# Splitting keys and values into float16 parts 1024 columns at a time

## The chip, the cores and the metric

The kernel runs on one core of a Trainium2 chip. The metric is the device time of one execution in microseconds; the time before is the median of three runs, 798.39 us (798.29 to 798.98).

## The reference

Block-sparse attention over four batches, eight heads, 768 positions and a head size of 64, followed by a gated MLP on the 3072 resulting tokens of 512 features. Each 32-row block of queries sees its neighbour blocks, the first and last block, and three drawn blocks; the first and last query blocks see everything. Cut to what matters:

```python
scores = scale * np.matmul(q, k.transpose(0, 1, 3, 2))
scores = np.where(mask, scores, -1000000000.0)
attn = softmax(scores)                     # with max subtracted, + 1e-09 in the divisor
x = np.matmul(attn, v)                     # heads joined: (3072, 512)
g = x @ w_gate                             # 512 -> 1536
out = (g * sigmoid(g) * (x @ w_val)) @ w_out   # 1536 -> 512
```

All inputs and the output are float32.

## The kernel before

TensorE multiplies float16. So every float32 operand is scaled by a power of two and split into two float16 parts: ACT writes the high part, `hi = scale * x` rounded to float16 (`hi_part`, line 391), and DVE the low part, `lo = scale * x - hi` (`lo_part`, line 394). A product is then three matmuls: high by high, high by low and low by high. Batch 0 and the first two of nine chunks of the MLP go in float32 as they are; batches 1 to 3 and the other chunks go in parts.

The work is staged so: while TensorE does the attention of batch 0 and its MLP chunks, ACT and DVE split the MLP's weights in place, `w1t` (gate and value) and `w2all` (output), one tile of 512 columns after the other (`split_w`). In a weight split the ACT instruction writes over what the split before it has still to read, so it waits for the DVE instruction of that split: the weight splits are a chain ACT, DVE, ACT, DVE. For each batch 1 to 3 `load_kv` then runs twice, for the values and for the keys:

- three loads of 256 tokens each into the buffer `stage` (four slots of 1024 float32 columns; a slot holds two tiles of 128 tokens by 512 columns), issued by the SP queue;
- a sum of squares on ACT (line 398), a matmul that sums it over the partitions (`nrm_v` or `nrm_k`, line 388), and on DVE the power-of-two scale (`vs` or `ks`);
- for each of three slots `i`, and in it for each of two halves `tt` of 512 columns, `high` on ACT and `low` on DVE. The parts of slot 0 go into the fourth slot, those of slot 1 into the slot that held the raw data of slot 0, and so on, so slot `i + 1` can be split only when slot `i` is done;
- values: one store of each split slot into a buffer in DRAM, `vd`, from which the attention gathers its rows. Keys: for each half a DMA that transposes it into `kst` (line 739), both issued by SP. DVE copies the key blocks of a query block from `kst` into `kring` (lines 1112 to 1115) ahead of its scores (`qk`, line 1137).

The attention of a block is a chain over all engines: scores on TensorE, maximum and mask on DVE (line 1151), exponential on ACT (line 1168), high and low parts of the probabilities (`pp`), a transposing DMA (`pts`, line 1193), the product with the values (`pv`, line 1206). TensorE fills the time between with matmuls of the MLP: `p` (line 1693, or 1687 in float32) and `po` (line 1756).

The order on each engine is set ahead. Every step is added to a `Plan` as a task with an engine, an estimated time, the tasks it needs, and a rank (shifted by a table, `SHIFT`); `Plan.order` plays the tasks through once with these estimates, and the instructions are emitted in that order. Each engine carries out its own instructions strictly in this order, waiting where it must. The tasks `high` and `low` of both halves stay in the plan with the estimates they had, so the order of tasks is the same with and without the change.

Of the kernel before, what the change touches and what calls it, by code (L numbers as in the profile page):

```python
# [17 lines left out]
B, H, S, D = 4, 8, 768, 64  # L18
# [101 lines left out]
class Plan:  # L120
# [9 lines left out]
    def add(self, eng, us, emit, need=(), rank=0.0, take=(), use=(), dma=None, behind=None, late=0.0, many=1):  # L130
        t = Task()
        t.late, t.many = late, many if dma is not None and eng != "POOL" else 0
        t.eng, t.us, t.emit, t.take, t.dma = eng, us, emit, list(take), dma
        t.key = self.key if rank > -50.0 else ""
        t.rank = rank + SHIFT.get(t.key, 0.0)
        t.need = [x for x in need if x is not None]
        t.outs, t.next, t.ready, t.end, t.no = [], [], 0.0, None, len(self.tasks)
        t.left = len(t.need) + (behind is not None)
        if behind is not None:
            behind.next.append(t)  # L140
        for x in t.need:
            x.outs.append(t)
        for b in list(take) + list(use):
            b.users.append(t)
        self.tasks.append(t)
        return t
# [81 lines left out]
def tile_block_sparse_attn_swiglu(  # L228
# [55 lines left out]
    def get(buf, name):  # L284
        if buf.ring in given:
            n = given[buf.ring]
            given[buf.ring] += 1
            buf.tile = stage[:, n % 4, :]
            return buf.tile
        pool, shape, dt, n = KINDS[buf.ring]  # L290
        buf.tile = pool.tile(shape, dt, tag=buf.ring, name=name, bufs=n)
        return buf.tile
# [97 lines left out]
    def hi_part(hi, src, scale):  # L390
        nc.scalar.activation(hi, src, AF.Copy, scale=scale)  # L391

    def lo_part(lo, src, scale, hi):
        nc.vector.scalar_tensor_tensor(lo, src, scale, hi, op0=ALU.mult, op1=ALU.subtract)  # L394
# [254 lines left out]
    def load_kv(b, what, rank, need):  # L649
# [4 lines left out]
        sc = {}  # L654
        raws, loads = [], []
# [41 lines left out]
        t = add("PE", 0.12, norm, sq, rank, take=[n])  # L697
        t = add("DVE", 0.7, scale, [t], EVAC, use=[n])
# [3 lines left out]
            bt.vsc, bt.vsc_t = sc, t  # L702
            bt.vd = dram.tile([S, 2 * DM], F16, tag="vd", name=f"vd_{b}")

        def views(i, tt):

            dst = parts[i].tile.bitcast(F16)
            pat = "p (t h l d) -> p t h l d" if what == "k" else "p (t l h d) -> p t h l d"
            dst = dst.rearrange(pat, h=H, l=2, d=D)
            return dst[:, tt, :, 0, :], dst[:, tt, :, 1, :], raws[i][1]().rearrange("p t (h d) -> p t h d", d=D)[:, tt]  # L710

        done = []
        for i in range(3):
            los = []
            for tt in range(2):

                def high(i=i, tt=tt):
                    if i and not tt:
                        get(parts[i], f"{what}16_{b}_{i}")
                    hi, _, s = views(i, tt)  # L720
                    hi_part(hi, s, sc["s"][:, 0:1])

                def low(i=i, tt=tt):
                    hi, lo, s = views(i, tt)
                    lo_part(lo, s, sc["s"][:, 0:1], hi)

                ru = [raws[i][0]]
                first = i > 0 and tt == 0
                pi = parts[i : i + 1]
                h_ = add("ACT", 0.63, high, [t] + los, rank, take=pi if first else [], use=ru + ([] if first else pi))  # L730
                l_ = add("DVE", 0.68, low, [h_], rank, use=ru + pi)
                los.append(l_)
                if what == "k":

                    def turn(i=i, tt=tt):
                        if i == 0 and tt == 0:
                            get(bt.ks, f"kst_{b}")
                        tok = (2 * i + tt) * P
                        nc.sync.dma_start_transpose(
                            bt.ks.tile[:, :, tok : tok + P],  # L740
                            parts[i].tile.bitcast(F16)[:, tt * 1024 : (tt + 1) * 1024],
                        )

                    f0 = i == 0 and tt == 0
                    done.append(add("SP", 1.3, turn, [l_], rank, behind=None if f0 else done[0], take=[bt.ks] if f0 else [],
                                    use=pi + ([] if f0 else [bt.ks]), dma=1.7))
            if what == "v":

                def put(i=i):
                    nc.sync.dma_start(  # L750
                        bt.vd[i * 256 : (i + 1) * 256, :].rearrange("(t p) n -> p t n", p=P),
                        parts[i].tile.bitcast(F16).rearrange("p (t n) -> p t n", t=2),
                    )

                done.append(add("SP", 0.5, put, los, rank, use=parts[i : i + 1], dma=1.6))
# [1099 lines left out]
```

## Time and profile before

| | |
|---|---|
| median of 3 runs | 798.39 us |
| profiled execution | 800.0 us, span 798.2 us |
| TensorE (PE) | 762.4 us busy, 96% of the span |
| VectorE (DVE) | 547.4 us, 69% |
| ScalarE (ACT) | 504.5 us, 63% |
| GpSimd (POOL) | 205.7 us, 26% |
| granted TensorE clock | 0.99 of full speed |
| splits of keys and values of batches 1 to 3 | 36 instructions on ACT, 36 on DVE, 25.2 and 27.2 us |

A row of the timeline reads: start in us from the span's start, duration in us, engine, line of the kernel, operation, output and inputs by the program's names, shapes, count, and in brackets the idle time of the engine before it with what ended it. A row of the groups gives count, busy time in us and the mean of one in ns, then idle time ahead of it. A row of the waits gives who waited for whom, the total in us, the number of times, and the longest. Matmuls overlap in TensorE's pipeline, so being busy is not the same as running at full rate.

### The profile page before, as it was taken

How to read it: one execution, taken by the hardware profiler on the slowest of the kernel's cores; microseconds unless marked ns; L12 is line 12 of the kernel's file. 1: busy time of each engine (PE TensorE's matmuls, PEld its weight loads, DVE VectorE, ACT ScalarE, POOL GpSimd, SP SyncE). 2: the span in 40 equal slices, each digit the busy share in tenths (PEclk: the TensorE clock that was granted, in tenths of full speed). 3: DMA queues.
4: the chain of work that ended last, by engine and by line, in shares of the span. 5: the costliest groups of instructions: out<-in, count | busy, mean ns of one | idle time of the engine just before them, and what ended most of it. 6: DMA issues, size and time to landing. Idle time of an engine off the chain costs nothing.

```text
span 798.2 us, 21196 instructions
## 1 busy us (share of the span) xinstructions
PE 762.4 (96%) x8098; PEld 489.2 (61%) x8098; DVE 547.4 (69%) x1658; ACT 504.5 (63%) x1211; POOL 205.7 (26%) x257
## 2 busy tenths in 40 slices
PE   3789999999999999999999999999999999999998
PEld 2557778884587566645665566645665566555655
DVE  5676898998898787742799866753798767731220
ACT  2687767587688686763598856754487757641221
POOL 3553511322033223201223222401223233101210
PEclk9889999999999999999999999999999999999999
DMA  8963537647877979478769994947878974330001
GB/s 205 259 220 118 193 146 260 205 125 230 198 151 172 212 169 197 91 197 265 159 134 182 269 227 114 203 97 211 188 133 179 228 177 105 69 69 19 1 1 39
DMA packets 171430, 128.08 MB, mean 160 GB/s; under 512 B 115008, under 2 KB 136896, under 8 KB 171328
## 3 DMA queue, kind: packets, MB, share of 16 engines
q1 hardware_dynamic: 165696, 109.42, 56.6%
q0 software_dynamic: 5632, 17.31, 8.5%
q8 instruction: 63, 1.03, 0.5%
q14 instruction: 39, 0.32, 0.1%
HBM read 79.50 MB, written 11.01 MB: 113 GB/s over the span
## 4 chain that ended last, share of the span: by engine, by line
PE 63%; DVE 18%; DMA 8%; issue 4%; ACT 4%; SPq 1%; DVEq 1%; ACTq 0%
PE p L1693 29%; PE po L1756 18%; PE pv L1206 4%; PE p L1687 3%; DMA q<-in_q_dram 3%; PE qk L1137 3%; DVE pp L394 2%; DVE act L1702 1%; DVE act L1707 1%; DMA pts<-pp 1%; DVE w1t L394 1%; DVE e L1151 1%; DMA stage<-in_k_dram 1%; DVE kring L1114 1%; PE qk L1341 1%
## 5 line engine op out<-in xcount | busy, mean ns | idle before, releaser
L1693 PE MATMUL p<-xall,w1t 128*128 128x384 f16 (+1 forms) x2016 | 326.8, 319 | 0.0
L1693 PEld LDWEIGHTS <-w1t 128*128 128x128 f16 x2016 | 191.2, 98 | 115.5 <-issue 8.5
L1715 POOL TENSOR_TENSOR h<-act,h 128x384 f16<-128x384 f32 (+1 forms) x108 | 101.6, 941 | 372.5 <-ACT h L1712 372.1
L1756 PE MATMUL po<-w2all,h 128*128 128x512 f16 (+1 forms) x900 | 195.3, 371 | 0.3 <-DVE w2all L394 0.3
L1756 PEld LDWEIGHTS <-h 128*128 128x128 f16 x900 | 84.6, 98 | 93.7 <-issue 5.6
L1712 ACT CAST h<-act 128x384 f16<-128x384 f32 (+1 forms) x108 | 50.8, 471 | 82.5 <-DVE act L1707 82.2
L1124 POOL DMA_INDIRECT w2all<-vd,vidx x66 | 62.8, 951 | 150.2 <-PE pv L1206 126.7
L1702 DVE SCALAR_TENSOR_TENSOR act<-act,p 128x384 f32<-128x384 f32 (+1 forms) x108 | 54.2, 504 | 65.2 <-ACT act L1698 64.5
L1687 PE MATMUL p<-xall,w1t 128*128 128x256 f32 x384 | 88.8, 384 | 0.4 <-DVE act L1702 0.3
L1168 ACT ACTIVATE e<-e,nb,es 128x256 f32<-128x256 f32 x132 | 78.2, 593 | 2.2
L1687 PEld LDWEIGHTS p<-xall,w1t 128*128 128x128 f32 x384 | 71.4, 192 | 12.0 <-DVE w2all L394 1.4
L1698 ACT ACTIVATE act<-p,gsc 128x384 f32<-128x384 f32 (+1 forms) x84 | 47.0, 560 | 31.2 <-PE p L1693 30.6
L1707 DVE SCALAR_TENSOR_TENSOR act<-act,hs,p 128x384 f32<-128x384 f32 (+1 forms) x84 | 49.7, 591 | 21.8 <-PE p L1693 18.8
L1206 PEld LDWEIGHTS <-w2all 128*128 128x128 f16 x1584 | 55.1, 98 | 13.9 <-issue 3.8
L394 DVE SCALAR_TENSOR_TENSOR pp<-e,rr,pp 128x256 f16<-128x256 f32 x132 | 61.2, 510 | 1.3 <-ACT pp L391 1.0
L391 ACT ACTIVATE pp<-e,rr 128x256 f16<-128x256 f32 x132 | 58.1, 496 | 3.7 <-DVE rr L782 2.5
L1206 PE MATMUL pv<-pts,w2all 128*128 128x64 f16 x1584 | 57.0, 193 | 2.8 <-DMA pts<-pp 2.8
L1151 DVE CUSTOM_DVE_ANT_1 e<-qk,msk 128x256 f32<-128x256 f32 x132 | 50.0, 417 | 2.8 <-issue 2.4
L1593 ACT ACTIVATE ot<-po,oc 128x512 f32<-128x512 f32 (+1 forms) x25 | 16.7, 667 | 42.9 <-PE po L1756 42.7
L1114 DVE COPY kring<-kst 128x256 f16 x198 | 38.9, 251 | 5.6 <-PE qk L1137 5.3
L1232 DVE TENSOR_TENSOR xall<-pv,xall 64x256 f16<-64x256 f32 x66 | 27.7, 420 | 21.1 <-ACT xall L1227 18.7
L1137 PE MATMUL qk<-kring,qs 128*32 128x256 f16 x1056 | 35.7, 274 | 0.2 <-DVE mx L1151 0.2
(187 smaller groups left out, 899.4 us busy)
## 6 DMA issues: line engine op xcount, KB each, us to landing
stage<-in_w_dram SPq DMA_DIRECT2D x36, 512.0 KB
w2all<-vd SPq DMA_DIRECT2D x66, 192.0 KB
qs<-qraw SPq DMA_DIRECT2D x72, 128.0 KB
out_dram<-ot SPq DMA_DIRECT2D x19, 256.0 KB
qn<-in_q_dram SPq DMA_DIRECT2D x36, 128.0 KB
qraw<-in_q_dram SPq DMA_DIRECT2D x36, 128.0 KB
stage<-in_v_dram SPq DMA_DIRECT2D x9, 512.0 KB
vd<-stage SPq DMA_DIRECT2D x9, 512.0 KB
```

Of the source, the lines that this page charges most:

```text
L391: nc.scalar.activation(hi, src, AF.Copy, scale=scale)
L394: nc.vector.scalar_tensor_tensor(lo, src, scale, hi, op0=ALU.mult, op1=ALU.subtract)
L1124: nc.gpsimd.indirect_dma_start(vf[0:96, 1, :], None, bt.vd, bass.IndirectOffsetOnAxis(ap=vidx[0:96, qb : qb + 1], axis=0))
L1137: nc.tensor.matmul(stv[u * BLK : (u + 1) * BLK, g].rearrange("p s k -> p (s k)"), o.q[:, l, h // 2, h % 2, col : col + BLK], kg[:, h].rear ...
L1151: nc.vector.tensor_tensor_reduce(ev[:, g], stv[:, g], o.g.msk[:, qb, :].unsqueeze(2).broadcast_to([P, 8, BLK]), scale=1.0, scalar=-3.0e38, ...
L1168: nc.scalar.activation(ev[:, g], ev[:, g], AF.Exp, bias=nb_[:, g : g + 1], scale=o.g.es[:, 0:1], accum_out=c["rs"][:, g : g + 1],)
L1206: nc.tensor.matmul(pvv[:, j, n % 2], vg[:, cc, l, 2 * j : 2 * j + 2, :], pq[:, g, m, cc, u : u + 2, :], start=i == 0, stop=i == 5,)
L1687: nc.tensor.matmul(t[:, 0:tc_], w[:, i + 1, k_ * P : (k_ + 1) * P], x_k(k_), start=k_ == 0, stop=k_ == NKT - 1)
L1693: nc.tensor.matmul(t[:, 0:tc_], w_[:, f, m, k_, :], x_k(k_, l), start=i == 0, stop=i == 11)
L1702: nc.vector.scalar_tensor_tensor(a_, a_, 1.0, pg.tile[:, 0:tc_], op0=ALU.add, op1=ALU.mult)
L1715: nc.gpsimd.tensor_tensor(hv(f)[:, 1, :], act.tile[:, 0:tc_], hv(f)[:, 0, :], op=ALU.subtract)
L1756: nc.tensor.matmul(po.tile[:, cs], hv(f)[:, l, ts_], w2h[:, f, m, cs], start=f == 0 and i == 0, stop=f == NF - 1 and i == 2)
```

## The change

`high` and `low` of the first half now take the whole slot, 1024 columns in one instruction; those of the second half emit nothing. The transposes and stores stay where they were, as do all other instructions. On SP the second transpose of a slot needs no wait of its own on DVE any more, since the first one has waited for the whole slot.

```diff
-        def views(i, tt):
+        def views(i):
...
-            return dst[:, tt, :, 0, :], dst[:, tt, :, 1, :], raws[i][1]().rearrange("p t (h d) -> p t h d", d=D)[:, tt]
+            return dst[:, :, :, 0, :], dst[:, :, :, 1, :], raws[i][1]().rearrange("p t (h d) -> p t h d", d=D)
...
                 def high(i=i, tt=tt):
                     if i and not tt:
                         get(parts[i], f"{what}16_{b}_{i}")
-                    hi, _, s = views(i, tt)
-                    hi_part(hi, s, sc["s"][:, 0:1])
+                    if not tt:
+                        hi, _, s = views(i)
+                        hi_part(hi, s, sc["s"][:, 0:1])
 
                 def low(i=i, tt=tt):
-                    hi, lo, s = views(i, tt)
-                    lo_part(lo, s, sc["s"][:, 0:1], hi)
+                    if not tt:
+                        hi, lo, s = views(i)
+                        lo_part(lo, s, sc["s"][:, 0:1], hi)
```

At two places the prediction shows what stands in a row on DVE: at the keys of batch 1 and at the values of batch 1.

## The prediction

> **What bounds the kernel now.** The first view read is the page: its busy line and its chain that ended last.
>
> ```profile
> PE 762.4 (96%) x8098; PEld 489.2 (61%) x8098; DVE 547.4 (69%) x1658; ACT 504.5 (63%) x1211; POOL 205.7 (26%) x257
> ...
> PE 63%; DVE 18%; DMA 8%; issue 4%; ACT 4%; SPq 1%; DVEq 1%; ACTq 0%
> ```
>
> TensorE is busy 96% of the span and carries 63% of the chain. The change removes nothing from it, so DVE and ACT time counts only where TensorE waits for them. The second view is the list of who waited, for TensorE.
>
> ```profile
> PE pv L1206 <- DMA pts<-pp: 2.8, 3, 1.3
> ...
> PE nrm_v L388 <- ACT stage L398: 2.4, 2, 1.3
> ...
> PE nrm_k L388 <- ACT stage L398: 1.6, 2, 1.3
> ...
> PE po L1756 <- DVE w2all L394: 0.3, 1, 0.3
> ```
>
> These are nearly all its waits after batch 0, 7.1 us together, and the most that a faster preparation could give back. Which of them can move is a matter of place, so the third view is TensorE in order of time.
>
> ```profile
> 188.94 4.48 PE L1756 MATMUL po<-w2all,h 128*128 128x512 f16 x20 [0.30 <-DVE w2all L394]
> ...
> 194.70 0.16 PE L388 MATMUL nrm_k<-kacc,ones_h 128*128 128x3 bf16 x1 [1.28 <-ACT stage L398]
> ...
> 214.24 1.06 PE L1137 MATMUL qk<-kring,qs 128*32 128x256 f16 x32
> ...
> 241.17 0.86 PE L1206 MATMUL pv<-pts,w2all 128*128 128x64 f16 x24 [1.34 <-DMA pts<-pp]
> ```
>
> All four belong to batch 1: its values are split around 170 to 182 us, its keys around 197 to 207, and its attention starts at 214. There the other engines are tight too, as the busy time by stretch of 20 us shows (PE, PEld, DVE, ACT, POOL).
>
> ```profile
> 220.00:240.00 20.00, 19.82 (x304) 17.03 (x296) 19.55 (x77) 17.80 (x54) 7.38 (x10) 1.00 0.75 152
> ```
>
> From 220 to 240 DVE is busy 19.55 of 20 us: whatever makes it late at 211 us is still late when the wait at 241.17 ends.
>
> **The price of a 1024-column instruction.** 36 instructions on each of ACT and DVE become 18. Groups by form:
>
> ```profile
> L391 ACT ACTIVATE stage<-stage,ks 128x512 f16<-128x512 f32 x18 | 12.6, 712 | 0.2 <-DVE ks L383 0.2
> ...
> L398 ACT ACTIVATE stage<-stage 128x1024 bf16<-128x1024 f32 x18 | 18.9, 1050 | 5.7 <-DMA stage<-in_v_dram 3.1 <-DMA stage<-in_k_dram 2.5
> ...
> L1632 ACT ACTIVATE sqx<-xall 128x1536 bf16<-128x1536 f16 x6 | 8.9, 1476 | 0.1
> ...
> L394 DVE SCALAR_TENSOR_TENSOR stage<-stage,vs 128x512 f16<-128x512 f32 x18 | 13.3, 750 | 2.6 <-ACT stage L391 2.6
> ...
> L432 DVE SCALAR_TENSOR_TENSOR w1t<-stage,w1t 128x1024 int32<-128x1024 int32 x12 | 14.7, 1224 | 0.3
> ```
>
> High part on ACT: 512 more columns cost 1476 - 1050 = 426 ns (squares), so 712 + 426 = 1.14 us, between 1.05 (the square itself) and 1.42 (two halves). Low part on DVE: between 1.22 (the 1024-column row) and 1.50 (two halves); I take 1.25, near the row with as many columns. Successive instructions overlap by about 0.08, so a half occupies 0.63 (ACT) or 0.66 (DVE), a whole 1.05 or 1.17. A merged pair thus frees 0.21 us of ACT and 0.15 of DVE, 3.8 and 2.7 us in 18 pairs. That is the whole saving.
>
> [...]
>
> **What it moves.** Every whole instruction stands where the first half stood, and is twice as long there. Beside the stage halves run the splits of the weights, w2all and w1t, each a chain by itself: the ACT part of one waits for the DVE part of the one before. On DVE at the keys of batch 1 (stage is the keys, w1t a weight split, kring the attention's first key gather), the last two of six pairs before:
>
> ```order
> L394 SCALAR_TENSOR_TENSOR stage<-stage,ks_2755 128x8x64
> L394 SCALAR_TENSOR_TENSOR w1t<-w1t,wsc 128x512
> L394 SCALAR_TENSOR_TENSOR stage<-stage,ks_2755 128x8x64
> L394 SCALAR_TENSOR_TENSOR w1t<-w1t,wsc 128x512 x3
> L1112 COPY kring_110<-kst_2781 128x16x32
> ```
>
> and all three after:
>
> ```order
> L394 SCALAR_TENSOR_TENSOR stage<-stage,ks_2749 128x16x64
> L394 SCALAR_TENSOR_TENSOR w1t<-w1t,wsc 128x512 x2
> L394 SCALAR_TENSOR_TENSOR stage<-stage,ks_2749 128x16x64
> L394 SCALAR_TENSOR_TENSOR w1t<-w1t,wsc 128x512 x2
> L394 SCALAR_TENSOR_TENSOR stage<-stage,ks_2749 128x16x64
> L394 SCALAR_TENSOR_TENSOR w1t<-w1t,wsc 128x512 x4
> L1114 COPY kring_110<-kst_2775 128x16x32
> ```
>
> Eight weight splits stand ahead of kring in both; one stage instruction per split became a double one per two splits. ACT changes alike. On DVE at the values of batch 1, the second part (act is the MLP's), before:
>
> ```order
> L394 SCALAR_TENSOR_TENSOR stage<-stage,vs_2527 128x512
> L394 SCALAR_TENSOR_TENSOR w2all<-w2all,oss 128x512
> L1702 SCALAR_TENSOR_TENSOR act_9_2587<-act_9_2587,p_9_2554 128x256
> L394 SCALAR_TENSOR_TENSOR stage<-stage,vs_2527 128x512
> L394 SCALAR_TENSOR_TENSOR w2all<-w2all,oss 128x512
> L1707 SCALAR_TENSOR_TENSOR act_9_2587<-act_9_2587,hw_112,p_9_2566 128x256
> ```
>
> and after:
>
> ```order
> L394 SCALAR_TENSOR_TENSOR stage<-stage,vs_2527 128x2x512
> L394 SCALAR_TENSOR_TENSOR w2all<-w2all,oss 128x512
> L1704 SCALAR_TENSOR_TENSOR act_9_2585<-act_9_2585,p_9_2553 128x256
> L394 SCALAR_TENSOR_TENSOR w2all<-w2all,oss 128x512
> L1709 SCALAR_TENSOR_TENSOR act_9_2585<-act_9_2585,hw_112,p_9_2564 128x256
> ```
>
> The first w2all now waits behind the whole part; the second follows without one.
>
> **The sum, keys of batch 1.** Rows of the timeline, ACT and then DVE:
>
> ```profile
> 196.72 0.72 ACT L391 ACTIVATE stage<-stage,ks 128x512 f16<-128x512 f32 x1
> ...
> 199.66 0.72 ACT L391 ACTIVATE w1t<-w1t,wsc 128x512 f16<-128x512 f32 x1 [0.71 <-DVE w1t L394]
> ...
> 200.86 0.71 ACT L391 ACTIVATE stage<-stage,ks 128x512 f16<-128x512 f32 x1
> ...
> 198.22 0.75 DVE L394 SCALAR_TENSOR_TENSOR stage<-stage,ks 128x512 f16<-128x512 f32 x1
> 198.88 0.75 DVE L394 SCALAR_TENSOR_TENSOR w1t<-w1t,wsc 128x512 f16<-128x512 f32 x1
> ...
> 202.27 0.75 DVE L394 SCALAR_TENSOR_TENSOR w1t<-w1t,wsc 128x512 f16<-128x512 f32 x1
> ...
> 205.35 0.75 DVE L394 SCALAR_TENSOR_TENSOR w1t<-w1t,wsc 128x512 f16<-128x512 f32 x1
> ...
> 208.44 0.75 DVE L394 SCALAR_TENSOR_TENSOR w1t<-w1t,wsc 128x512 f16<-128x512 f32 x1 [0.79 <-ACT w1t L391]
> 209.98 0.75 DVE L394 SCALAR_TENSOR_TENSOR w1t<-w1t,wsc 128x512 f16<-128x512 f32 x1 [0.79 <-ACT w1t L391]
> 210.86 0.29 DVE L1112 COPY kring<-kst 128x512 f16<-128x512 f16 x1
> ```
>
> The last w1t rows stand 1.54 apart with nothing else on DVE: the w1t chain (0.72 + 0.75 + two handovers) sets the pace, and the halves fit into its 0.79 us shadows. The whole ones don't. First: the low part starts at 198.22 as before (its high part ends at 197.9) and holds DVE 0.51 longer, so the split at 198.88 goes to 199.39, ACT's at 199.66 to 200.17, the high part at 200.86 to 201.37. Second: that ends at 202.51, the low part runs from 202.55, and the split at 202.27 starts at 203.72, 1.45 late. Third: the next ACT split is at 204.51, the high part 205.14 to 206.28, the low part from 206.32, and the split at 205.35 starts at 207.49, 2.1 late. Nothing behind it on DVE is shortened, so kring goes from 210.86 to 213.0: +2.1.
>
> The transposes of the keys are six DMAs on SP as before. The first waits for the whole low part, so it and the second, and the store behind them, go later; the last two are issued at 207.6 and about 208.9. Their landing took
>
> ```profile
> 206.80 3.97 DMA kst<-stage
> ```
>
> in the chain of waits, so 212.9, level with DVE: no further cost.
>
> **The sum, values of batch 1.** The same with the w2all chain, ACT and then DVE:
>
> ```profile
> 169.57 0.72 ACT L391 ACTIVATE stage<-stage,vs 128x512 f16<-128x512 f32 x1
> ...
> 173.08 0.72 ACT L391 ACTIVATE w2all<-w2all,oss 128x512 f16<-128x512 f32 x1
> ...
> 176.79 0.72 ACT L391 ACTIVATE w2all<-w2all,oss 128x512 f16<-128x512 f32 x1
> ...
> 180.99 0.72 ACT L391 ACTIVATE w2all<-w2all,oss 128x512 f16<-128x512 f32 x1 [0.82 <-DVE w2all L394]
> ...
> 170.56 0.74 DVE L394 SCALAR_TENSOR_TENSOR stage<-stage,vs 128x512 f16<-128x512 f32 x1
> ...
> 176.01 0.74 DVE L394 SCALAR_TENSOR_TENSOR w2all<-w2all,oss 128x512 f16<-128x512 f32 x1
> ...
> 179.80 1.16 DVE L394 SCALAR_TENSOR_TENSOR w2all<-w2all,oss 128x512 f16<-128x512 f32 x1
> ...
> 181.94 0.74 DVE L394 SCALAR_TENSOR_TENSOR w2all<-w2all,oss 128x512 f16<-128x512 f32 x1
> ```
>
> The first low part starts 0.19 late (170.75) and holds DVE 0.51 longer, so all behind it is 0.7 late; the removed half would give 0.66 back, but the next DVE w2all needs ACT's at 173.08, now 173.77, and stays 0.5 late. By the same steps the second whole makes the DVE split at 176.01 start at 177.36 (+1.35), ACT's at 176.79 at 178.13; the third puts DVE's at 179.80 to 181.44. If that one takes 0.74 (its 1.16 were a slowed one), ACT's at 180.99 goes to 182.21 and DVE's at 181.94 to 182.97: +1.0. From there DVE is full, so the split that TensorE waits for at 188.94 and the squares of 194.70 come 1.0 late. The keys' load only needs the values' store, now a little earlier.
>
> Together 1.0 + 2.1 = 3.1 us at kring, with bounds of 2.6 (the short prices worked through alike) and 5.3 (nothing saved by merging). TensorE's key scores at 214.24 have slack (the first two key blocks are copied by 213.4), but the DVE chain behind is full until the wait at 241.17, apart from small gaps such as
>
> ```profile
> 217.33 0.42 DVE L1151 CUSTOM_DVE_ANT_1 e<-qk,msk 128x256 f32<-128x256 f32 x1 [0.32 <-issue]
> ```
>
> whose releaser isn't shown. I let it absorb its 0.3, and take 2.8.
>
> **Batches 2 and 3: nothing.** No weights are split there. The places nearest to hurting:
>
> ```profile
> 392.96 0.29 DVE L1112 COPY kring<-kst 128x512 f16<-128x512 f16 x1 [1.60 <-DMA kst<-stage]
> ...
> 396.49 1.06 PE L1137 MATMUL qk<-kring,qs 128*32 128x256 f16 x32
> ...
> 356.78 1.47 ACT L1632 ACTIVATE sqx<-xall 128x1536 bf16<-128x1536 f16 x1
> ...
> 358.71 0.81 PE L1637 MATMUL xn<-sqx,ones_h 128*128 128x384 bf16 x4
> ```
>
> Keys of batch 2: I put the last transpose 0.7 later, so the copies from 393.7; two of 0.9 us each, which the scores need, end at 395.5, ahead of 396.49: TensorE's matmuls before it are the cover. Values of batch 2: the second high part, longer by 0.42, pushes the square at 356.78 by 0.3, to 358.55, just ahead of 358.71. Elsewhere TensorE's list names no wait on these splits. The saving is covered too: 12 of 18 pairs lie under TensorE's own work.
>
> **The rivals.** (1) Faster: freed engine time decides. If the weight chains had room, the keys' own chain of six pairs (0.71 + 0.75 + handovers = 1.53 each) would become three of 2.46, 1.8 us less, and the attention would start earlier: the waits at 188.94 and 241.17 would go, -1.6 us to -1.8, 796.7. It decides if the w1t split behind a whole instruction is less than 0.3 us late; the 1.54 period with idle DVE speaks against. [...]
>
> (2) No change: TensorE's slack takes the keys' part. Its scores have 0.9 us, and if the wait at 241.17 is set by the SP queue and not by DVE, only the 1.0 from the values remains: 799.4. DVE's 19.55 of 20 speaks against.
>
> (3) Slower than forecast: TensorE in batches 2 and 3 loses its small margins (0.16 us at 358.71), or low parts are slowed like the 1.16 row: +0.4 to +1.5, up to 802.7.
>
> That the change doesn't do what it says is out: one instruction of 128x16x64 or 128x2x512 stands per part.
>
> **How the numbers follow.** The profiled execution took 800.0 us for a span of 798.2; the median of the runs is 798.39, and the 2.8 us are added to that: 801.2. A difference under 0.2% (1.6 us) can't be told from none. Forecast (with rival 3) 0.66, its own range 800.0 to 803.0; no change 0.22, between 797.5 and 800.0; faster 0.12. So slower 0.66, same 0.22, faster 0.12. The range from 798.4 to 803.0 leaves out the faster rival and the tails, about 2 in 10.
>
> **What would show it.** Right: 18 whole groups of about 1.14 us on ACT and 1.25 on DVE; in the keys of batch 1 w1t rows on DVE some 2.8 us apart across a stage row instead of 1.54 to 1.85; kring about 3 us later; TensorE's wait for w2all near 189 us longer by about 1 us, a new wait at the first key scores and longer ones up to 241; the rest of the time line shifted by a constant. Wrong: kring at 211 or earlier, a last w2all split near 182, or new TensorE waits beyond 260 us.

## Result and the profile after

The changed kernel is slower, by more than the prediction's range allowed: a median of 803.3 us over twelve executions (798.88 to 809.14) against 796.78 us for the kernel before on the same chip (792.82 to 798.98), a ratio of 1.0088 with a 95% interval from 1.0069 to 1.0106, or +7.0 us (5.5 to 8.4). The direction was forecast, the size was not: 2.8 us were expected. A second run of the same kernel gave 1.0099 (1.0066 to 1.0132).

The profiled execution of the first run took 809.14 us for a span of 807.3, the slowest of its twelve. So it holds more than the change does; what belongs to the change is separated from chance below, by seventeen profiles of fifteen kernels. The line of the page with the engines' busy times, and those lines of TensorE's waits that bear on batch 1 (total over the whole kernel, number of times, longest one):

```profile
PE 765.2 (95%) x8098; PEld 489.8 (61%) x8098; DVE 545.2 (68%) x1640; ACT 501.2 (62%) x1193; POOL 208.1 (26%) x257
```

```profile
PE pv L1208 <- DMA pts<-pp: 6.2, 5, 3.3
PE nrm_v L388 <- ACT stage L398: 3.6, 2, 2.5
...
PE nrm_k L388 <- ACT stage L398: 2.0, 2, 1.5
PE p L1689 <- DVE act L1704: 1.4, 2, 1.1
PE qk L1139 <- DVE kring L1117: 1.1, 1, 1.1
...
PE po L1758 <- DVE w2all L394: 0.6, 1, 0.6
```

New in batch 1 are the waits for act (the MLP's float32 chunk, near 175 us) and for kring (the first key scores, as forecast); the wait for pts near 241 us is 3.3 us instead of 1.34, and w2all's 0.6 instead of 0.30. Line numbers from about 720 on are one or two higher than before.

**The values of batch 1.** DVE's rows of the timeline after the change (start, duration, and in brackets the idle time before and who ended it), then TensorE's:

```profile
172.27 1.28 DVE L394 SCALAR_TENSOR_TENSOR stage<-stage,vs 128x1024 f16<-128x1024 f32 x1 [0.24 <-ACT stage L391]
173.47 1.16 DVE L394 SCALAR_TENSOR_TENSOR w2all<-w2all,oss 128x512 f16<-128x512 f32 x1
174.56 0.41 DVE L1704 SCALAR_TENSOR_TENSOR act<-act,p 128x256 f32<-128x256 f32 x1
```

```profile
175.02 1.78 PE L1689 MATMUL p<-xall,w1t 128*128 128x256 f32 x7 [1.11 <-DVE act L1704]
186.63 4.48 PE L1758 MATMUL po<-w2all,h 128*128 128x512 f16 x20 [0.55 <-DVE w2all L394]
192.60 0.16 PE L388 MATMUL nrm_k<-kacc,ones_h 128*128 128x3 bf16 x1 [1.50 <-ACT stage L398]
```

The second whole low part (1.28 us) waits for its whole high part, then stands ahead of a weight split and of act, which frees the buffer `p` that TensorE's next matmul writes. Counted from the squares of the values (`nrm_v`, 167.22 us before, 163.27 after), act ended at 9.87 us before, 0.6 ahead of TensorE; now it ends at 11.70, and TensorE stands for 1.11 us in this list.

The weight split behind the whole low part takes 1.16 us here, where most take 0.74. GpSimd's product `h` runs at the same time, here and at the third whole low part, whose weight split (178.01 us) takes 1.16 us too:

```profile
173.22 0.86 POOL L1717 TENSOR_TENSOR h<-act,h 128x256 f16<-128x256 f32 x1 [4.60 <-ACT h L1714]
177.68 0.94 POOL L1717 TENSOR_TENSOR h<-act,h 128x256 f16<-128x256 f32 x1 [3.60 <-ACT h L1714]
```

So it is in all seventeen profiles: from 140 us on, the 1002 low parts of 512 columns on DVE that have no such product beside them take at most 0.77 us, and all 87 that take more than 1 us overlap one. No run moved the product alone, so this is a coincidence in time and not a tested cause.

**The keys of batch 1.** DVE, first pair to kring, with a gap of rows before the last two, and ACT's rows of the first pairs:

```profile
196.12 1.28 DVE L394 SCALAR_TENSOR_TENSOR stage<-stage,ks 128x1024 f16<-128x1024 f32 x1
197.32 0.74 DVE L394 SCALAR_TENSOR_TENSOR w1t<-w1t,wsc 128x512 f16<-128x512 f32 x1
198.85 0.75 DVE L394 SCALAR_TENSOR_TENSOR w1t<-w1t,wsc 128x512 f16<-128x512 f32 x1 [0.79 <-ACT w1t L391]
200.47 1.29 DVE L394 SCALAR_TENSOR_TENSOR stage<-stage,ks 128x1024 f16<-128x1024 f32 x1 [0.86 <-ACT stage L391]
201.67 0.75 DVE L394 SCALAR_TENSOR_TENSOR w1t<-w1t,wsc 128x512 f16<-128x512 f32 x1
...
210.06 0.75 DVE L394 SCALAR_TENSOR_TENSOR w1t<-w1t,wsc 128x512 f16<-128x512 f32 x1 [0.79 <-ACT w1t L391]
210.73 0.29 DVE L1114 COPY kring<-kst 128x512 f16<-128x512 f16 x1
```

```profile
194.62 1.15 ACT L391 ACTIVATE stage<-stage,ks 128x1024 f16<-128x1024 f32 x1
198.10 0.72 ACT L391 ACTIVATE w1t<-w1t,wsc 128x512 f16<-128x512 f32 x1 [1.72 <-DVE w1t L394]
199.30 1.14 ACT L391 ACTIVATE stage<-stage,ks 128x1024 f16<-128x1024 f32 x1
```

Across the second stage row the w1t rows stand 2.82 us apart (198.85 to 201.67) and across the third 2.25, instead of 1.54 to 1.85. The second low part waits 0.86 us for its high part, which itself stood behind a late weight split: while the prediction's picture was a busy DVE, there is idle time in it too, since each engine waits for the other's long instruction. kring is copied 18.13 us after the squares of the keys (210.73 - 192.60) instead of 16.16.

**From the first scores to the probabilities.** TensorE's row of the first scores, and then for the kernel before and the changed one the SP transpose of the probabilities, GpSimd's gather of values nearest to it, and the product that waits for the transpose:

```profile
213.28 1.16 PE L1139 MATMUL qk<-kring,qs 128*32 128x256 f16 x32 [1.07 <-DVE kring L1117]
```

```profile
236.25 1.23 SPq L1193 DMA_TRANSPOSE pts<-pp  x1
236.78 0.92 POOL L1124 DMA_INDIRECT w2all<-vd,vidx  x1 [0.87 <-PE pv L1206]
241.17 0.51 PE L1206 MATMUL pv<-pts,w2all 128*128 128x64 f16 x12 [1.34 <-DMA pts<-pp]
```

```profile
236.02 1.23 SPq L1195 DMA_TRANSPOSE pts<-pp  x1
236.17 0.92 POOL L1126 DMA_INDIRECT w2all<-vd,vidx  x1 [0.49 <-PE pv L1208]
242.54 0.69 PE L1208 MATMUL pv<-pts,w2all 128*128 128x64 f16 x10 [3.32 <-DMA pts<-pp]
```

From the transpose's issue to the product it takes 4.92 us before and 6.52 after: not only does it start 0.73 us later against the first scores (22.74 us after them instead of 22.01), it also takes 1.6 us longer. GpSimd's gather, which TensorE's earlier product releases, comes 0.53 us behind the transpose before, and 0.15 behind it after.

**The clock.** The rows by stretch (busy times of PE, PEld, DVE, ACT and POOL with instructions, granted TensorE clock, DMA share, GB/s) of the changed kernel's first profile:

```profile
230.00:238.00 8.00, 8.00 (x151) 7.09 (x149) 7.93 (x29) 7.02 (x21) 3.58 (x5) 1.00 0.85 179
...
241.00:245.00 4.00, 2.46 (x30) 2.18 (x31) 1.97 (x9) 3.22 (x11) 0.75 (x1) 0.60 0.73 147
245.00:250.00 5.00, 5.00 (x86) 4.17 (x84) 2.64 (x14) 2.80 (x7) 1.51 (x3) 0.98 0.25 76
```

A clock of 0.60 over the 4 us from 241 and of 0.98 over the next 5 is 3.4 us at half speed (1.6 and 0.1 us lost of 4 and 5). It begins at 241.83 us, while TensorE still waits. Of eleven profiles with a wait of about 2.5 us or more at this place seven show it. What tells them apart stands in the traces: in each profile the lowered stretches ahead of the span's end last 3.41 us or a multiple of it, and their starts lie whole multiples of 3.41 us apart (in this one a second stretch, also at 0.50, starts at 354.47 us, 112.64 or 33 times 3.413 us behind the first). The span can so be cut into windows of 3.41 us. Two of them in the changed kernel, and two of the same kind in keys1, an experiment below:

```profile
238.42:241.83 3.41, 0.79 (x8) 0.46 (x5) 3.35 (x14) 2.01 (x7) 1.36 (x2) 1.00 1.48 163
241.83:245.24 3.41, 2.70 (x31) 2.33 (x32) 1.16 (x7) 2.42 (x9) 0.97 (x2) 0.50 0.70 182
```

```profile
233.18:236.59 3.41, 2.35 (x40) 1.93 (x37) 3.36 (x12) 1.30 (x4) 1.52 (x3) 1.00 0.80 72
236.59:240.00 3.41, 1.70 (x34) 1.63 (x35) 3.00 (x14) 2.70 (x10) 0.89 (x2) 1.00 1.17 286
```

In the changed kernel TensorE is busy for 0.79 us of one window, so idle for 2.62, and the next window has the clock of 0.50. In keys1 the wait of 2.77 us falls into two windows, 1.06 and 1.71 us idle, and the clock stays at 1.00. At this place the seven profiles with a lowered clock had 2.1 to 3.0 us of idle time in one window, and the ten without had at most 1.7. So the length of the wait alone does not tell them apart (2.53 us in changedagain with the lowered clock behind it, 2.77 in keys1 without), but the idle time in one window does, and where the windows lie against the kernel differs from profile to profile (one starts at 241.83 us here, one at 236.59 in keys1). No run moved the windows alone, so this separates seventeen profiles and is not a tested cause.

### The profile page after: what moved, and what is told of

Read it like the earlier page. It is cut to its first block, busy times and chain, and to the rows that moved or that the text cites. A ratio compares the mean times of both kernels' runs of the same rounds, so it can differ in the third digit from the quotient of the medians.

```text
span 807.3 us, 21150 instructions
## 1 busy us (share of the span) xinstructions
PE 765.2 (95%) x8098; PEld 489.8 (61%) x8098; DVE 545.2 (68%) x1640; ACT 501.2 (62%) x1193; POOL 208.1 (26%) x257
```

## Experiments

Every run is compared with runs of the kernel before on its own chip, whose medians lay between 795.5 and 801.9 us; so ratios are compared, not times. What each profile shows of batch 1 is in this table, in us, all worked out from the rows of the timeline as above. Lead is the time from the issue of the pts transpose on SP to GpSimd's gather; negative where the gather came first.

| kernel | squares of values to those of keys | keys' squares to kring | to first scores | lead | transpose issued to product | ratio to before (95%) |
|---|---|---|---|---|---|---|
| before | 27.48 | 16.16 | 19.54 | 0.53 | 4.92 | |
| beforeagain | 27.48 | 16.39 | 19.54 | 0.29 | 4.92 | 1.0011 (0.9987 to 1.0036) |
| batches23 | 27.48 | 16.21 | 19.54 | 0.49 | 4.87 | 1.0005 (0.9977 to 1.0033) |
| keys1 | 27.49 | 18.13 | 20.68 | -0.21 | 5.61 | 1.0025 (0.9995 to 1.0055) |
| values1 | 29.32 | 16.44 | 19.54 | -0.11 | 6.23 | 1.0030 (0.9997 to 1.0063) |
| values1late | 28.63 | 16.40 | 19.54 | -0.06 | 6.15 | 1.0061 (1.0043 to 1.0079) |
| batch1 | 29.75 | 18.13 | 20.68 | 0.13 | 5.71 | 1.0066 (1.0037 to 1.0096) |
| high1 | 27.42 | 16.95 | 19.60 | 0.14 | 5.94 | 1.0004 (0.9978 to 1.0031) |
| low1 | 29.81 | 18.64 | 21.29 | 0.13 | 6.66 | 1.0058 (1.0031 to 1.0086) |
| place1 | 28.78 | 17.71 | 20.26 | 0.15 | 5.73 | 1.0044 (1.0021 to 1.0068) |
| copytwice | 27.49 | 16.29 | 19.54 | 0.13 | 6.01 | 0.9995 (0.9973 to 1.0018) |
| copythrice | 27.48 | 16.35 | 19.64 | 0.15 | 5.66 | 1.0022 (0.9995 to 1.0048) |
| copyhold | 27.47 | 15.98 | 19.54 | 0.94 | 4.94 | 1.0021 (0.9993 to 1.0050) |
| changed | 29.33 | 18.13 | 20.68 | 0.15 | 6.52 | 1.0088 (1.0069 to 1.0106) |
| changedagain | 29.31 | 18.13 | 20.68 | 0.14 | 5.72 | 1.0099 (1.0066 to 1.0132) |
| changedhold | 29.32 | 18.13 | 20.69 | 0.69 | 4.65 | 1.0078 (1.0049 to 1.0107) |
| planned | 29.12 | 17.50 | 19.54 | 0.19 | 5.44 | 1.0170 (1.0127 to 1.0213) |

In profiles of the same kernel TensorE's stretches up to the first scores repeat to 0.02 us and the copy into kring to 0.23, though whole executions scatter by 0.2 to 0.5% (standard deviation): this made single profiles worth more than medians here. Between kernels that do the same up to there the difference can be larger: batch1 has 29.75 us where the changed kernel has 29.33. A profile is one execution: for batch1 and values1late it is the fastest of the run, for the first run of the changed kernel the slowest.

### Which load: keys1, values1, batch1, batches23

One condition on top of the changed kernel; where it is false, the halves are done as before. (The second line stands for four kernels.)

```diff
+        whole = b == 1 and what == "k"      # keys1
+        # values1: b == 1 and what == "v"; batch1: b == 1; batches23: b > 1
...
-                    if not tt:
-                        hi, _, s = views(i)
+                    if not whole or tt == 0:
+                        hi, _, s = views(i, None if whole else tt)
```

> Only the keys of batch 1 are split 1024 columns at a time; all other splits stay at 512. Theory A (the weight-split chain of the keys of batch 1 carries the loss, as predicted): kring of the first key scores goes from 210.9 to about 213 us, counted from where the squares of the keys end, and the time rises by 2.1 us (+0.26%). Theory B (batches 2 and 3 carry most): the same kring, but the excess is gone by the wait at 241 us, less than +1 us. Theory C (a longer TensorE wait also costs clock): as A, and the wait for the pts transfer at 241 us is over 2.4 us with a granted clock under 1.00 in the 10 us behind it, together +3 to +4 us (+0.4 to +0.5%).

> Only the values of batch 1 are split 1024 columns at a time. Theory A: +1.0 us (+0.13%), since the last w2all split comes 1.0 later and what follows with it. Theory B: 0. Theory D (seen in the profile of the changed kernel): TensorE also waits about 1.3 us near 175 us for a bank of the MLP that DVE frees behind a whole low part; as the w2all splits are late by the same DVE, this is not added to the 1.0 but takes its place, +1.3 to +1.7 us (+0.2%).

> Keys and values of batch 1 are split 1024 columns at a time, those of batches 2 and 3 stay at 512. Theory A: the whole loss is here; by the prediction's sum +2.8 to +3.1 us, and by the profile of the changed kernel, in which batch 1 lost 6 us, +6 us (+0.75%). Theory B: +3 us (+0.4%), and the rest of the 7 us belongs to the other two batches. Theory C: at least one TensorE wait over 2.4 us in batch 1 with a granted clock of about 0.83 behind it; without one the loss stays at 3 to 4 us.

> Keys and values of batches 2 and 3 are split 1024 columns at a time, those of batch 1 stay at 512. Theory A: no change (within 0.2%), as predicted. Theory B: +2 to +4 us (+0.25 to +0.5%), with TensorE waits of the kind seen in the changed kernel: for the squares of the values of batch 2 near 350 us over 2.4 us with a clock of 0.83 behind it, new ones at the key scores near 415 us (DVE's row maxima) and at xn near 459 us. If those two waits are chance of single runs, they are missing here and the time is that of before.

Measured: 1.0025, 1.0030, 1.0066 and 1.0005, so +2.0, +2.4, +5.2 and +0.4 us of 795.5. Theory A holds in its place: batch 1 carries the loss, and batches 2 and 3 together carry none that can be told. In batch 1 TensorE has no wait for act in batches23 (the one in its list, 1.6 us, lies at 143 us, ahead of the splits of batch 1). At the squares of the values it waits 1.1 us in batch 1 and 0.8 in batch 2, together in its list:

```profile
PE nrm_v L388 <- ACT stage L398: 1.9, 2, 1.1
```

So the wait of 2.5 us there in the first profile was chance, and theory B falls. Theory C is half right: keys1 and batch1 had waits of 2.8 and 2.5 us without a lowered clock, values1 one of 3.3 us with it. keys1 shows the forecast kring (+1.97 us) and the wait of 1.1 us at the first scores. values1 shows what the prediction had not: TensorE reaches the squares of the keys 1.84 us later, 1.1 of it the wait for act, and then loses 1.9 us more at pts (against the first profile of the kernel before), although the first scores come without a wait.

### Which engine: high1, low1

high1 does ACT's part whole and DVE's in halves, in batch 1 only; low1 the reverse, with ACT's two halves one after the other ahead of DVE's whole.

```diff
 # low1
-                    hi, _, s = views(i, tt)
-                    hi_part(hi, s, sc["s"][:, 0:1])
+                    for u in range(2) if not tt else ():
+                        hi, _, s = views(i, u)
+                        hi_part(hi, s, sc["s"][:, 0:1])
...
+                    if not tt:
+                        hi, lo, s = views(i, None)
+                        lo_part(lo, s, sc["s"][:, 0:1], hi)
```

> In batch 1 only ACT's high parts are 1024 columns (in the place of the first half); DVE's low parts stay at 512 in their places, and batches 2 and 3 stay at 512. Theory V (DVE's longer hold carries the loss): no wait of 1.27 us near 175 us, the squares of the keys at most 0.8 us later against those of the values (28.3 us), kring at most 0.9 us later, +0 to +2 us. Rival (ACT's longer hold carries it, since the weights' next split waits for ACT): kring 1.5 us or more later and the squares of the keys over 1.3 us later, +4 to +5 us as with both engines.

> In batch 1 only DVE's low parts are 1024 columns; ACT does both halves one after the other in the place of the first (two instructions of 0.72 us instead of one of 1.15), and batches 2 and 3 stay at 512. Theory V (DVE's longer hold carries the loss; the run with ACT alone lost nothing): TensorE's wait of 1.27 us near 175 us is back, the squares of the keys come 29.3 us or more after those of the values, kring 18.1 us or more after the squares of the keys, and the time is +5 to +7 us as with both engines. Rival (only the two together lose): squares of the keys at 28 us or less, kring at 17.2 us or less, +2 us or less.

high1: 1.0004, with no wait for act in batch 1. low1: 1.0058, and its two waits are longer than in the changed kernel:

```profile
PE qk L1152 <- DVE kring L1130: 1.7, 1, 1.7
PE p L1702 <- DVE act L1717: 1.8, 2, 1.5
```

DVE's hold carries the loss; ACT's longer instruction alone costs TensorE nothing up to the first scores (19.60 against 19.54 us), though kring is 0.8 us later. In low1 DVE waits for 2 x 0.72 us of ACT instead of 1.15, and TensorE is later than in the changed kernel at every mark; in the whole time the two can't be told apart (their intervals overlap).

### Which place: place1, values1late

place1 keeps 512 columns but does the second half right behind the first, on both engines. values1late does the values of batch 1 whole in the place of the second half.

```diff
 # place1, both engines alike
+                    for u in range(2) if not tt else ():
+                        hi, lo, s = views(i, u)
+                        lo_part(lo, s, sc["s"][:, 0:1], hi)
 # values1late, both engines alike
+                    if whole:
+                        if tt:
+                            hi, lo, s = views(i, None)
+                            lo_part(lo, s, sc["s"][:, 0:1], hi)
```

> In batch 1 all instructions stay 512 columns wide, but the second half's stand right behind the first half's, in the place of the first; batches 2 and 3 as before. DVE then holds 2 x 0.75 us less the overlap, about 1.42, where the whole instruction holds 1.28. Theory M (the merge loses as a reorder: the second half is pulled ahead of the weights' split and of the MLP's act, and the width itself only saves): as with DVE alone or worse: TensorE's wait near 175 us 1.6 us or more, the squares of the keys 29.8 us or more after those of the values, kring 18.6 us or more after the squares of the keys, and +6 to +8 us (+0.75 to +1.0%). Rival (the wide instruction itself is what loses, whatever its place): TensorE as before, 27.5 and 16.2 us, and less than +2 us.

> As the run with the values of batch 1 alone, but each whole instruction stands in the place of the second half instead of the first. Theory P (the place decides: a whole low part ahead of the MLP's act instruction keeps TensorE's bank): the wait of 1.27 us near 175 us is gone, and from the squares of the values to the squares of the keys TensorE takes 27.5 to 28.5 us instead of the 29.3 with the first place (27.48 before); +0 to +1.5 us in all. Rival (the length decides, wherever it stands): 29.3 us and a wait of over 1 us somewhere in this stretch, +2.4 us as with the first place.

place1 gave 1.0044: theory M is right in kind and its numbers were too high. Without any wide instruction, pulling the second half ahead of the weight split costs TensorE 1.30 of the 1.85 us up to the keys' squares, kring 1.55 of 1.97, and the first scores 0.72 of 1.14. TensorE's wait near 175 us is 0.44 us there, where the theory had 1.6 or more. The rest of the loss fits with a whole low part that can't start before a whole high part ends: with halves DVE starts on the first half 0.2 us earlier (3.34 against 3.53 us after the squares). No run separates this part. In values1late the wait for act is gone and 0.9 us for w2all stands in its place, 28.63 us against 29.32: between the two theories. Its time (1.0061) is no better than with the first place (1.0030, intervals overlapping). A later place moves the wait, it doesn't end it.

### The order of two queues: copytwice, copythrice, copyhold, changedhold, beforeagain

copytwice and copythrice are the kernel before with one 0.29 us copy on DVE done two or three times. copyhold and changedhold add work to GpSimd in batch 1, on its sixth gather only, in copytwice and in the changed kernel.

```diff
 # copytwice (copythrice: 3)
-                nc.vector.tensor_copy(kg[:, :, 3:8:4, :], two[:, :, 0 : NB : NB - 1, :])
+                for _ in range(2 if b == 1 and not once else 1):
+                    nc.vector.tensor_copy(kg[:, :, 3:8:4, :], two[:, :, 0 : NB : NB - 1, :])
 # copyhold, changedhold
+            gone.append(b)
+            if b == 1 and gone.count(1) in (6,):
+                nc.gpsimd.memset(vf[0:96, 1, 0:512], 0.0)
             nc.gpsimd.indirect_dma_start(
```

> The kernel before, with the first copy into kring of batch 1 (0.29 us on DVE) made twice, and nothing else. Theory F (a flip of order between two queues): the transpose of the probabilities (pts) that TensorE waits for near 241 us is issued on SP 22.0 us after the first key scores, 0.5 us ahead of GpSimd's gather of values; 0.29 us more on DVE made it 0.64 us later in the kernel with whole values, behind the gather, and its landing took 6.1 us instead of 4.8. So here too: TensorE's wait there goes from 1.3 to about 3.2 us, +1.9 us (+0.24%) for 0.29 us of work. Rival (no flip; the wait grows by what DVE is late): a wait of 1.6 to 1.9 us, +0.3 to +0.6 us, not told from no change.

> The run with the copy made twice, and GpSimd's sixth gather of values of batch 1 (22.6 us after the first key scores) put off by a memset of its own target ahead of it (both wait for the same release). Theory F (the gather on the other queue slows the transpose): the transpose, issued on SP at 22.5 as in that run, lands in 4.8 us instead of about 5.8, and TensorE's wait falls from 2.8 to about 1.8 us although GpSimd has more to do. Rival (the transpose waits for something else): the wait stays at 2.6 us or more. In the time this is at most 1 us, within what can be told.

> The changed kernel with the same memset ahead of GpSimd's sixth gather of batch 1. Theory F: TensorE's wait for pts falls from 3.3 us to 1.6 to 2.2 us, no lowered clock behind it, and the time is 1 to 2.5 us under the changed kernel's: +4.5 to +6 us over before (+0.55 to +0.75%). Rival: the wait stays, and the time is +7 us (+0.88%) or more.

> The kernel before once more, unchanged, for the scatter of single profiles. If the short wait of the first profile is typical: TensorE's wait for pts near 74 us after the squares of the values is 1.2 to 1.6 us again, the transpose it waits for is issued on SP about 22.0 us after the first key scores and lands within 5 us, and there is no stretch of lowered clock behind it. If it was luck: a wait of 2.5 us or more. Time: within 0.2% of before.

> The kernel before with the first copy into kring of batch 1 made three times (0.58 us more on DVE). Theory F: the transpose is issued on SP 22.6 to 22.9 us after the first scores, at most 0.2 us ahead of GpSimd's gather or behind it, lands in 5.5 us or more, and TensorE waits 2.7 us or more. If that wait is a real loss, the time is +1.5 to +2.5 us (+0.2 to +0.3%), and the run with the copy made twice was a chance within its interval. Rival (a later stretch gives it back): wait as said, but the time within 0.1% of before.

In changedhold DVE, ACT and SP do what they do in the changed kernel, and the transpose is issued at the same 22.75 us after the first scores. Only the gather is later:

```profile
237.99 1.23 SPq L1199 DMA_TRANSPOSE pts<-pp  x1
237.88 0.52 POOL L1129 MEMSET w2all<- 96x512 f16 x1 [0.24 <-PE pv L1212]
238.68 1.08 POOL L1130 DMA_INDIRECT w2all<-vd,vidx  x1 [0.27 <-POOL w2all L1129]
242.64 0.54 PE L1212 MATMUL pv<-pts,w2all 128*128 128x64 f16 x13 [1.47 <-DMA pts<-pp]
```

With 0.69 us of lead the product comes 4.65 us after the issue instead of 6.52 and 5.72, the wait is 1.47 us, and the clock in the 4 us from 241 is 1.00:

```profile
241.00:245.00 4.00, 2.53 (x50) 2.06 (x52) 3.97 (x17) 2.84 (x9) 2.30 (x3) 1.00 0.92 178
```

More work on GpSimd took 1.1 to 1.9 us off TensorE's wait. copyhold points the same way (1.53 us of wait, where copytwice has 2.84), but its transpose was also issued 0.3 us earlier than in copytwice (22.17 against 22.47 us after the first scores), so it is the weaker test. beforeagain repeats the short wait, 1.58 us, and copythrice has 2.46, a little under what was expected.

That the wait hangs on the gather's start is shown by changedhold, and the table agrees: the five profiles with a lead of 0.29 us or more have 4.65 to 4.94 us, the eleven with 0.15 or less have 5.61 to 6.66, and the one with 0.19 (planned, below) has 5.44. How the gather makes the product later, and why the turn lies between 0.15 and 0.29 us of lead, no run shows.

What this wait is worth in the whole time is less sure. In single profiles it is plain: from the squares of the values of batch 1 to those of batch 2 changedhold takes 186.86 us, the changed kernel 190.04 and 189.57, the kernel before 183.00 and 182.89. In the whole times it is not: changedhold's 1.0078 lies above what theory F gave it (at most 1.0075) and under the rival's 1.0088, and its interval holds both. copytwice and high1, whose products came 1.3 to 1.8 us later and with a lowered clock behind them, gave 0.9995 (at most +1.4 us) and 1.0004 (at most +2.5), and copythrice 1.0022 (+1.7, from -0.4 to +3.8). Together these say 0 to 2 us; whether some of it is given back behind batch 1 stays open.

### The change once more, and with a planner that knows it: changedagain, planned

> The changed kernel once more, unchanged, for the scatter of single profiles. What belongs to the change is here again: 29.3 us from the squares of the values to those of the keys, kring at 18.1 us, the first scores 20.7 us after the squares of the keys, the transpose on SP 22.7 us after them and 0.15 us ahead of GpSimd's gather, with a wait of 2.5 to 3.3 us. What was chance of that one run is gone: the wait of 2.5 us for the squares of the values of batch 2 with the lowered clock behind it, and the loss behind 420 us. Time: +5 to +7 us over before.

1.0099, and the expected marks to about 0.02 us; the time, +7.9 us, is above the expected +5 to +7. Rows of TensorE in beforeagain (first two) and changedagain, the squares of the values of batch 1 and of batch 2:

```profile
165.19 0.17 PE L388 MATMUL nrm_v<-vacc,ones_h 128*128 128x3 bf16 x1 [1.12 <-ACT stage L398]
...
348.08 0.16 PE L388 MATMUL nrm_v<-vacc,ones_h 128*128 128x3 bf16 x1 [1.28 <-ACT stage L398]
```

```profile
162.33 0.17 PE L388 MATMUL nrm_v<-vacc,ones_h 128*128 128x3 bf16 x1 [1.10 <-ACT stage L398]
...
351.90 0.16 PE L388 MATMUL nrm_v<-vacc,ones_h 128*128 128x3 bf16 x1 [1.39 <-ACT stage L398]
```

Between the two rows lie 182.89 and 189.57 us: +6.7 us in batch 1. TensorE's last matmul ends 447.0 and 447.4 us behind the second row: +0.4 in all that follows. The wait of 2.5 us in batch 2 did not come again.

planned keeps the whole instructions but tells the planner their length:

```diff
-                h_ = add("ACT", 0.63, high, ...
-                l_ = add("DVE", 0.68, low, ...
+                h_ = add("ACT", 0.02 if tt else 1.06, high, ...
+                l_ = add("DVE", 0.02 if tt else 1.21, low, ...
```

> The changed kernel, with the planner told of the real shape: 1.06 us on ACT and 1.21 us on DVE for the place of the first half, 0.02 us for the empty second one, instead of 0.63 and 0.68 twice. TensorE's order stays as it is; ACT, DVE, SP and GpSimd are reordered around the loads of batch 1. Theory O (an order planned for halves is what loses): DVE's act near 175 us is moved ahead of the low part, the wait of 1.27 us there is gone, kring is copied at 16 to 17 us after the squares of the keys instead of 18.1, and the time is within 2 us of before (799 us or less). Rival (whole instructions in the shadow of the weights' splits lose in any order): still 3 to 5 us above before.

1.0170 (1.0127 to 1.0213), the slowest of all. The expectation was wrong in its premise too: the other engines were reordered in all of batches 1 to 3, not only around batch 1's loads, and TensorE's order stayed only into batch 2; from there, where the squares of the values of batch 3 now come earlier, it changed too. Batch 1 was little better than in the changed kernel (squares of the keys at 29.12 us, kring at 17.50), and a new wait stands in batch 2:

```profile
464.40 0.32 PE L1695 MATMUL p<-xall,w1t 128*128 128x384 f16 x1 [3.09 <-ACT xall L1229]
```

So the theory that a planner's wrong estimate is the cause finds no support; as a test it is unclean, since it moved so much in batches 2 and 3. No experiment points to a version faster than the kernel before: ACT alone whole, and batches 2 and 3 whole, cost and gain nothing that can be told.

## Why the prediction was wrong in size

Three steps of its sum failed: the term of the values of batch 1 was too small, the wait at 241 us was taken to grow only by what DVE is late, and the clock behind that wait had no term.

**Batches 2 and 3: right.** Predicted nothing; +0.4 us in batches23 and +0.4 behind batch 1 in changedagain.

**Keys of batch 1, the chain: right.** kring +2.1 us forecast, +1.97 measured; first scores, with TensorE's slack of 0.9 us taken off, +1.2 by the prediction's numbers, +1.14 measured. The reasons held: the w1t chain has no room behind a longer DVE instruction. Whole instructions took 1.15 and 1.28 us in batch 1, where 1.14 and 1.25 were taken.

**Values of batch 1: +1.0 forecast, +1.85 measured.** This is the first step that failed. Two things were missed. The prediction moved everything on DVE behind the second whole part by 1.35 us, and by its own rows the act instruction with it; but it did not ask who waits for act. TensorE did, with a margin of 0.6 us, so its own 1.35 would have given a wait of 0.75; act came 1.83 late and the wait was 1.11. And the prediction let the last w2all split win back time from a 1.16 us row taken as a slowed one; such slow rows came behind the second and the third whole part (1.16 us at 173.47 above, and at 178.01), so nothing was won back: the last split stands 1.97 us later against the squares of the values, where 1.0 was forecast. All of these rows overlap a product of GpSimd, an engine that the prediction left out.

**From the first scores to pts: passing DVE's delay on one for one was the second step that failed.** By the prediction's numbers DVE would be 0.9 us late against TensorE (3.1 less 1.0 and 1.2), and with the 0.3 that it let a gap absorb, the wait at 241 us would grow by 0.6. DVE was 0.8 us late at kring, as forecast, but the wait grew by 1.0 to 2.0 us (1.34 and 1.58 us in the two profiles before, 3.32 and 2.53 in the two after): the transpose came 0.5 to 0.7 us later on SP's queue, which took its lead over the gather from 0.53 and 0.29 us to 0.15 and 0.14. The time from the issue to the product changed with that lead (4.92 us in both profiles before, 6.52 and 5.72 after), and the prediction treated it as fixed. The price in the trace of batch 1 is shown; in the whole time it lies within 0 to 2 us, as said.

**The clock: missed.** A longer wait at 241 us lowered it in both profiles of the changed kernel, for 3.4 us at half speed. That can lose at most 1.7 us (half of 3.41); over the work behind the product that takes the kernel before 3.1 us, up to the second row of `p`, the changed kernel fell behind by a further 1.3 us (first profile) and 1.6 (second). In the seventeen profiles the clock was lowered where 2.1 us or more of idle time lay in one window and not where it was 1.7 or less, and waits of like length (2.53 and 2.77 us) fell on either side, so a forecast could have given this term only a chance.

The sum with what was measured, for changedagain against beforeagain: 1.83 to the squares of the keys, 1.14 at the first scores, 1.30 at pts, 1.6 of clock, together 5.9 of the 6.7 us of batch 1. Matched matmul by matmul, TensorE then wins back 0.6 us, and loses 1.3 us near 331 us, where waits of its scores for ACT make 0.8 in the list of waits; why they came was not tried.

**The rivals.** Faster (1) and no change (2) are out. In (3) the mechanism named, small margins of batches 2 and 3, did not decide; of its slowed low parts one came (the first of the keys of batch 3, 1.94 us in batches23 and in both profiles of the changed kernel), in a place where batches23 shows no loss, and slowed weight splits came in batch 1. What was listed as signs came: 18 whole groups, w1t rows 2.8 us apart, a longer wait for w2all (by 0.25 us, not by 1, since the wait for act stands ahead of it), a new one at the first scores. A sign of being wrong came too, new TensorE waits beyond 260 us (near 331 us in the second profile); but the second profile of the kernel before has one that the first lacks, 1.69 us at 378 us, so that sign could not tell. kring was forecast "about 3 us later" on one scale; it is 1.85 + 1.97 = 3.8 us later, counted from the squares of the values.

place1 adds to the reasons for the slower kernel: equally small instructions lose most of the same when they stand together (1.30 of 1.85 us up to the keys' squares, 1.55 of 1.97 at kring), so what the halves buy here is the other work between them.

## What to carry to other kernels

Merging two instructions of an engine that carries out its own in a set order is a reorder: the second half is pulled ahead of everything that stood between (in place1, without any wide instruction, this cost 1.30 us up to the keys' squares), and each of those has someone waiting, so ask it of every instruction passed over, not only of those in the chain that is looked at. Busy time saved (2.2 us on DVE and 3.3 on ACT) said nothing here, where a chain with idle shadows of 0.79 us set the pace. And where a wait ends with a DMA, look at what the other queues issue within half a microsecond of it: here a few tenths on the engine before it went with the step from 4.65 to 4.94 us between issue and product (a lead of 0.29 us or more) to 5.61 to 6.66 (0.15 or less).

## What was not expected of the hardware

- A pts transpose issued on SP at most 0.15 us ahead of a gather issued by GpSimd was followed by its product 5.61 to 6.66 us later (eleven profiles); with 0.29 us or more of lead, 4.65 to 4.94 us (five); with 0.19, 5.44 (one).
- A wait of TensorE of 2.5 to 3.5 us at one place was followed by 3.4 us of half clock (0.50) in seven of eleven profiles. In these seven, 2.1 to 3.0 us of idle time lay within one window of 3.41 us; in the ten without a lowered clock there, at most 1.7.
- 512-column low parts that take 0.74 us took 1.16 at some places (173.47 and 178.01 us above, 179.80 in the kernel before). Every low part over 1 us, 87 in the seventeen profiles from 140 us on, overlaps a product of GpSimd; without one beside them 1002 took at most 0.77.
